# A fused attention and gated feed-forward kernel: a buffer of its own, three early sums, another order and engine table

## The chip, the cores and the metric

The kernel runs on one core of a Trainium2 chip. The metric is the device time of one launch in microseconds (us). The median of three runs of the kernel before is 399.03 us (398.22, 399.34 and 399.03).

The core's engines each work through their own queue in order: TensorE (PE in the profile; PEld are its weight loads), VectorE (DVE), ScalarE (ACT), GpSimd (POOL) and SyncE (SP). Here POOL also issues the loads, and SP most of the stores.

## The reference

Attention with a squared relu in place of the softmax, then a gated feed-forward block. Eight batches, twelve heads, 448 tokens, head size 64; model width 768, inner width 1536.

```
scores = q @ k.T / sqrt(64)
attn   = relu(scores)**2 / 448
x      = attn @ v                      # heads side by side: 3584 tokens x 768
g, val = x @ w_gate, x @ w_val
out    = (gelu(g) * val) @ w_out
```

Inputs and output are float32; the kernel computes in bfloat16 and sums in float32.

## The kernel before

**Matmuls.** All the kernel's matmuls but transposes, warm-up and fillers work on a 64 x 64 quarter of the array (`mm`, L408). A step (`Op`) is two matmuls beside each other in columns; the steps for the upper rows of the array form one lane (PE0), those for the lower rows another (PE1). When both lanes have work, four quarter matmuls run at once.

**Attention of a batch.** The heads of a batch come in six pairs, and two pairs make a third: third (b, m) is heads 4m to 4m+3 of batch b. For the first two batches PE turns q and k by transposes (`add_first_transposes` L632, `add_transposes` L658), DVE or ACT copies them out of PSUM (L647, L680). A batch has 21 scores steps u (`add_scores`, L706): PE multiplies into one of two PSUM buffers, a relu reads it (L743, ScalarE), a square follows on VectorE (L752). `add_values` (L782) multiplies by v and writes the scaled result to xT (L814 VectorE, L825 ScalarE).

**Feed-forward.** `add_gate_value` (L1040) makes one sum for 128 inner columns fc and for the gate (g = 0) or the value (g = 1): six steps in each lane over the six 128-row pieces of x, then a Gelu (L1061) or a product (L1066). The weights come in six chunks of 256 inner columns (w0 to w5), a gate and a value half each. For some columns (those of chunk 2 in batches 0 and 1) two batches are worked together by seven products in place of eight (`add_pair`, L926, with weight sums made on VectorE, L890). The output product (`add_product`, L1193) does the same for tiles of tokens. In the last two batches the products at L990 may run on GpSimd.

**Order.** The program is planned at build time. Batch 0 has a fixed order: a list of (time, step) entries, where score u stands at `lo + u * step`, so that places can be told in scores. All later work is a list of units in the order of `LINE` (L12); `run_plan` (L107) goes through time, takes the first unit that can begin, and gives each operation of ACT, DVE and GpSimd to its engine, or, where it has an alternative (`other`), to the engine that can begin first. Where the plan leaves PE idle before 30 us, `fill` (L583) puts in matmuls whose result nobody reads (L597), but only into banks that have been used before.

**Start.** A zeroed tile (L395) feeds eight pairs of warm-up matmuls (L1465). GpSimd issues the first loads and makes the identity matrix for the transposes (a memset and a mask) behind the first two.

**Loads.** All run through GpSimd's queue, in order. `LOADS` (L31) is the order after batch 0: w a weight chunk, o a quarter of the output weights, q a third of q and k, v a third of v. q and k land in a ring of two buffers (`hpool`, RING_H), v in one of three: a load waits until the transposes, or the values, of the third that used its buffer are done (L1469).

**The first batch's sums.** The gate and the value sum of fc = 0 are in batch 0's fixed list (L1045, L1371): three upper-row steps each before the last values, three behind; their lower-row steps follow later.

## Time and profile before

| | |
|---|---|
| runs of the kernel before | 398.22, 399.34, 399.03 us; median 399.03 |
| profiled execution, first to last instruction (span) | 396.5 us, mean granted TensorE clock 0.998 |
| batch 0's attention | from 5.6 to about 27.2 us of the span |
| last matmul's end, end of the span | 391.3, 396.5 us |

The profiled execution's own total isn't listed with the three runs; its span of 396.5 us leaves out what lies before the first and behind the last instruction. In the views, a line has the engine, the line of the kernel (a helper's line, where one helper issues all: L409 is every quarter matmul), the operation, what it writes and reads, its form and count, then busy us and mean ns, then idle time of the engine before it and what ended that. In rows of stages each engine has its busy us and, in brackets, its count; the last three columns are the granted clock, the DMA engines' share and GB/s. In a timeline the columns are start, length, and what ran. The chain of work that ended last is followed back from the last instruction.

### The profile page before, as it was taken

What the parts mean: (1) busy time and instruction counts of PE and PEld (TensorE: products, weight loads), DVE (VectorE), ACT (ScalarE), POOL (GpSimd) and SP (SyncE); (2) the same over time, 40 slices, a digit from 0 to 9 for tenths busy, and PEclk for the clock granted to TensorE, in tenths of its full rate; (3) what the DMA queues carried; (4) which work ended last, traced back from release to release, by engine and by line L of the source; (5) the groups of instructions that cost most, each with busy time, mean ns of one, the idle gap of its engine ahead of it and who ended that gap; (6) DMA issues with size and microseconds to landing.
All of it is one profiled execution on the core that took longest, in us unless ns stands there. A gap on an engine that the chain in (4) does not pass through costs nothing.

```text
span 396.5 us, 18486 instructions
## 1 busy us (share of the span) xinstructions
PE 388.8 (98%) x8414; PEld 329.9 (83%) x8414; DVE 313.0 (79%) x540; ACT 256.2 (65%) x388; POOL 96.5 (24%) x142
## 2 busy tenths in 40 slices
PE   8999999999999999999999999999999999999994
PEld 3555868888989997888999979999999977779993
DVE  2885897698977778889887879898988897688642
ACT  4957873787777656785776658778877465554220
POOL 8548423061230130120300402210110034341100
PEclk9999999999999999999999999999999999999999
DMA  7999999799796694573879997657523320000136
GB/s 99 180 192 175 197 195 143 96 148 155 103 233 108 113 192 71 87 95 51 110 140 150 141 196 122 89 86 120 75 30 83 94 70 4 3 2 3 41 104 180
DMA packets 75054, 44.38 MB, mean 112 GB/s; under 512 B 34400, under 2 KB 71520, under 8 KB 74976
## 3 DMA queue, kind: packets, MB, share of 16 engines
q0 software_dynamic: 38784, 24.39, 45.3%
q1 hardware_dynamic: 35792, 18.03, 22.9%
q8 instruction: 66, 1.08, 1.1%
q10 hardware_dynamic: 400, 0.79, 0.6%
q14 instruction: 12, 0.10, 0.1%
HBM read 48.76 MB, written 11.01 MB: 151 GB/s over the span
## 4 chain that ended last, share of the span: by engine, by line
PE 97%; ACT 1%; issue 0%; DVE 0%
PE ff L409 85%; PE sp L409 9%; PE ff L597 1%; PE sp L676 1%; PE ff L1465 1%; PE ff L676 1%; ACT attnT L743 1%; PE ff L639 0%; ACT qkT L647 0%; ACT osb L1267 0%; ACT xT L825 0%; DVE held L395 0%; DVE table L398 0%
## 5 line engine op out<-in xcount | busy, mean ns | idle before, releaser
L743 ACT ACTIVATE attnT<-sp 128x896 bf16<-128x896 f32 x168 | 151.3, 921 | 46.6 <-PE sp L409 44.0
L409 PE MATMUL ff<-xT,wg 64*64 64x448 bf16 x1680 | 174.5, 349 | 0.0
L409 PE MATMUL ff<-xT,wv 64*64 64x448 bf16 x1056 | 112.5, 349 | 0.0
L409 PEld LDWEIGHTS <-wv 64*64 64x64 bf16 x1680 | 93.5, 107 | 13.4 <-issue 0.6
L409 PEld LDWEIGHTS <-wg 64*64 64x64 bf16 x1680 | 93.6, 107 | 10.9
L752 DVE TENSOR_TENSOR attnT<-attnT 128x1792 bf16<-128x1792 bf16 (+1 forms) x98 | 92.2, 953 | 10.5 <-ACT attnT L743 10.0
L409 PE MATMUL ff<-attnT,v 64*64 64x448 bf16 (+1 forms) x768 | 81.5, 326 | 0.1
L409 PE MATMUL sp<-qkT 64*64 64x448 bf16 (+1 forms) x768 | 74.3, 328 | 0.9 <-ACT qkT L647 0.6
L409 PE MATMUL ff<-ts,wv 64*64 64x448 bf16 x624 | 69.3, 349 | 0.0
L409 PEld LDWEIGHTS <-s 64*64 64x64 bf16 x1200 | 66.8, 107 | 2.6 <-issue 0.2
L486 POOL DMA_DIRECT2D v<-in_v_dram x48 | 30.4, 648 | 104.2 <-ACT attnT L743 51.2
L981 DVE TENSOR_TENSOR part<-ff,part 128x448 f32<-128x448 f32 x78 | 47.0, 621 | 9.1 <-PE ff L409 6.3
L409 PE MATMUL ff<-ts,ws 64*64 64x448 bf16 x480 | 54.0, 349 | 0.0
L409 PE MATMUL ff<-wt,s 64*64 64x384 bf16 x624 | 52.1, 323 | 0.0
L409 PEld LDWEIGHTS <-uT 64*64 64x64 bf16 x912 | 50.6, 107 | 1.1
L409 PE MATMUL ff<-wo,s 64*64 64x384 bf16 x576 | 50.9, 323 | 0.0
L409 PE MATMUL ff<-wo,uT 64*64 64x384 bf16 x576 | 49.8, 323 | 0.0
L409 PEld LDWEIGHTS <-v 64*64 64x64 bf16 x768 | 44.0, 107 | 5.0 <-issue 0.9
L409 PEld LDWEIGHTS <-ws 64*64 64x64 bf16 x720 | 41.3, 106 | 5.7 <-issue 0.3
L409 PEld LDWEIGHTS <-qkT 64*64 64x64 bf16 x768 | 35.2, 106 | 9.3 <-issue 4.4
L977 ACT COPY part<-ff 128x448 f32<-128x448 f32 x54 | 28.8, 533 | 20.6 <-PE ff L409 19.4
L471 POOL DMA_DIRECT2D qk<-in_q_dram x26 | 16.5, 633 | 101.2 <-DVE attnT L752 37.7
(76 smaller groups left out, 499.7 us busy)
## 6 DMA issues: line engine op xcount, KB each, us to landing
out_dram<-osb SPq DMA_DIRECT2D x51, 192.0 KB, 3.2
v<-in_v_dram POOLq DMA_DIRECT2D x48, 128.0 KB, 4.9
qk<-in_q_dram POOLq DMA_DIRECT2D x22, 224.0 KB, 5.5
qk<-in_k_dram POOLq DMA_DIRECT2D x22, 224.0 KB, 5.8
wg<-in_moe_w_gate_dram POOLq DMA_DIRECT2D x6, 384.0 KB, 9.6
wv<-in_moe_w_val_dram POOLq DMA_DIRECT2D x6, 384.0 KB, 10.7
wo<-in_moe_w_out_dram POOLq DMA_DIRECT2D x8, 288.0 KB, 7.7
out_dram<-osb ACTq DMA_DIRECT2D x3, 192.0 KB, 3.4
```

The costliest lines, as they stand in the source:

```text
L409: return nc.tensor.matmul(o, lhsT, rhs, start=start, stop=stop, skip_group_check=onto, tile_position=(P * row, P * col))
L471: op = load(4 * (h1 - h0) * S * D, lambda: nc.gpsimd.dma_start(tile_of(), src[b, h0:h1].rearrange("h (p c) d -> p h (c d)", c=SC)), deps, ...
L486: return nc.gpsimd.dma_start(v16[b, m][HALF[i], :, :, :], v[b, h0:h1].rearrange("h (p c) d -> p h c d", c=SC)[:, :, c0:c0 + VC, :])
L597: nc.tensor.matmul(t[:, :], warm[:, 0:128], warm[:, :], start=True, stop=True)
L676: nc.tensor.transpose(t[HALF[j], c, :], src[:, 2 * r + j, c, :], ident[:, :], tile_position=(0, P * j))
L743: relu.ins = nc.scalar.activation(duo["a"][:, u % 2, :, :], box[0][:, :, 0:S], AF.Relu).ins
L752: nc.vector.tensor_tensor(a[:, part], a[:, part], a[:, part], op=ALU.mult)
L977: rd.ins = copy(st["t", name][:, :], box[0][:, 0:S]).ins
L981: rd.ins = nc.vector.tensor_tensor(t[:, :], box[0][:, 0:S], t[:, :], op=ALU.add).ins
L1465: nc.tensor.matmul(t[HALF[j], :], warm[:, HALF[j]], warm[:, :], start=True, stop=True, tile_position=(0, P * j))
```

## The change

It has these parts.

- **Start.** The warm-up reads the constant 1.0 instead of the zeroed tile and has ten pairs instead of eight. `fill` may also use a bank that nothing has used yet, and counts on half the pace before 7.2 us; it thus adds a matmul ahead of the first scores. The identity's memset goes to VectorE, its mask behind the second pair of loads.
- **Own buffer.** q and k of third (0, 2) land in a tile of another pool (`lpool`) and take no turn in the ring of two; the turns of all later thirds move up by one.
- **Loads.** `LOADS` now names each load; the order is another one.
- **Three early sums.** Gate of fc 0, gate of fc 1 and value of fc 0 stand in batch 0's list, with a place for each step (`SUMS_AT`: fc, g, lane that goes first, six places in scores). The sum of fc 1 does its lower rows first.
- **Order.** Batch 0's transposes and values have places of their own (`TURN_AT`, `VALUE_AT`), and `LINE` is another order of the same units.
- **Engines.** More operations have an alternative: relus of the first two batches (VectorE), squares (ScalarE, in batch 0 GpSimd for every third u), copies of batch 0's transposes and xT (ScalarE), the copies that regroup q and k (ScalarE). A table, `CHOICE`, says for each of 373 operations whether it stays (0), goes to the other engine (1), or is left to the plan (a dot). In order of the operations the table begins with batch 0's 21 relus, `1010.00.001.01...000.`; for batch 0 it fixes the squares of u = 8, 9 and 14 on ScalarE and that of u = 13 on GpSimd and leaves eight open; for batches 1 to 7 it fixes 14 squares on ScalarE.
- **The plan's figures.** Durations, load times and start times in the plan are other ones, and it keeps VectorE and GpSimd apart for some operations. These act through the order alone. (`NP4`, `SPANS`, `BY_DVE`, `ALONE_FROM` and `SOON_V` have values that change nothing.)

A copy of both transposes of a third in batch 1 and later also waits for both, not for its own alone.

The diff, cut to its core:

```diff
-w q q w q v q w v w w v w q v q o v q o q v o o q v v q v v v q q v q v q v q q q v v q q v v q q v
-v v
+w0 q10 q11 w1 w5 q12 v10 v12 v11 w3 w4 q20 q21 v20 w2 v21 q22 o3 q30 o2 q31 o1 v22 o0 v31 q32 v30
+q40 v32 v40 q41 q42 q51 q50 v41 v50 v42 v51 q52 v52 q60 v60 q61 q62 q70 v62 v61 q71 q72 v70 v72 v71
...
+TURN_AT = (-1.3, 2.0, 4.2, 6.5, 11.2, 13.5)
+VALUE_AT = (7.2, 9.2, 13.2, 16.2, 19.2)
+TURN1_AT = 23.61
+SUMS_AT = ((0, 0, 0, 18.4, 20.7, 21.0, 22.8, 23.0, 25.5), (1, 0, 1, 21.0, 21.2, 22.0, 22.0, 23.3, 27.8), (0, 1, 0, 21.0, 21.1, 21.8, 21.9, 24.8, 25.75))
...
+    nc.vector.memset(ident[:, :], 0.0)
...
+    def qk_tile(b, m):
+        if (b, m) not in qk16:
+            home, name = (lpool, "qkr") if (b, m) == (0, 2) else (hpool, "qk16")
+            qk16[b, m] = home.tile([128, 4, SC * D], bf16, name=name, tag=name)
+        return qk16[b, m]
...
-        if t1 > FILL:
+        if t1 > FILL or not held:
             return
-        at_rest = {k: -1.0 if r is None else r.end for k, r in held.items() if r is None or r.end is not None}
+        at_rest = {k: -1.0 if held.get(k) is None else held[k].end for k in range(FB)
+                   if held.get(k) is None or held[k].end is not None}
...
-        n = int((t1 - t0 - 0.15) / 0.22)
+        n = int((t1 - t0 - 0.15) / (0.22 if t1 > COLD else 0.43))
...
-        relu = Op("ACT", 0.845, emit_relu, [ops[0][-1], ops[1][-1]], lag=0.18, prio=2)
+        relu = Op("ACT", 0.845, emit_relu, [ops[0][-1], ops[1][-1]], lag=0.18, prio=2,
+                  other=("DVE", 1.0, emit_relu) if b < EARLY else None)
...
+            sq = Op("DVE", 0.575 if alone else 1.05, emit_sq, [relu] if alone else duo["relu"], lag=0.2, prio=2,
+                    other=("GPS", 1.75, lambda: emit_sq(nc.gpsimd)) if aside
+                    else ("ACT", 0.85 if alone else 1.5, lambda: emit_sq(nc.scalar)))
...
-        if h0 == 0:
-            POOL.append(Op("POOL", 0.6, lambda: make_identity(nc, ident)))
+        if h0 == 2:
+            POOL.append(Op("POOL", 0.3, lambda: make_identity(nc, ident, nomemset=True)))
...
-    work += [(0.0, 5, add_gate_value, (0, 0, g)) for g in range(2)]
+    soon = {(0, fc, g): (fore, *(lo + x * step for x in at)) for fc, g, fore, *at in SUMS_AT}
+    for key, at in soon.items():
+        work.append((at[1], 5, lambda t, key, end: kept.__setitem__(key, take_bank(t, end - t + 12.0)), (key, at[-1])))
+        work.append((0.0, 5, lambda _, key, at: add_gate_value(at, *key), (key, at)))
...
     def emit_warm_up():
+        ones = nc.const_aps.tensor(1.0, (128, 512), bf16)
         t = new_bank(0, None)
-        for _ in range(8):
+        for _ in range(10):
             for j in range(2):
-                nc.tensor.matmul(t[HALF[j], :], warm[:, HALF[j]], warm[:, :],
+                nc.tensor.matmul(t[HALF[j], :], ones[:, HALF[j]], ones,
...
-        for new, old in zip(thirds[ring:], thirds):
+        turns = [x for x in thirds if made is not qk_loads or x != (0, 2)]
+        for new, old in zip(turns[ring:], turns):
...
+    either = [op for op in [*ACT, *DVE, *SP] if op.other is not None]
+    free_to = {"ACT": [*ACT], "DVE": [*DVE], "GPS": [*GPS], "SP": [*SP]}
+    picks = "".join(CHOICE.split()) or [op.choice for op in either]
+    for op, pick in zip(either, picks):
+        op.choice = pick
+        if pick == "1":
+            free_to[op.engine].remove(op)
+            op.engine, op.cost, op.emit = op.other
+        if pick != "0":
+            free_to[op.other[0]].append(op)
```

More of the change, by code (lines that the diff above doesn't have):

```diff
@@ L52, in __init__ @@
         self.open = False
+        self.choice = "."
+        self.port = self.full = False
+        self.first = engine, cost
 class Ring:
@@ L104 @@
 ALONE = True
+BEGIN = {"PE0": 1.2, "PE1": 1.2, "POOL": 1.25, "GPS": 1.25, "ACT": 2.3, "DVE": 1.4, "SP": 0.75}
+MOVED = 0.0
 def run_plan(queues, pools, units, banks, arrivals, together, fill):
-    free = {e: 0.0 for e in (*queues, *pools)}
+    free = {e: BEGIN.get(e, 0.0) for e in (*queues, *pools)}
     at = {e: 0 for e in queues}
-    dma = last = floor = busy = alone = 0.0
+    dma = MOVED
+    last = floor = busy = alone = 0.0
+    port = {"DVE": 0.0, "GPS": 0.0}
     fixed = len(queues["PE0"])
@@ L282, in run_plan @@
         free[e] = op.end
+        if op.full:
+            free["PE1"] = op.end
+        if op.port and e in port:
+            port[e] = op.end
+        if e in ("POOL", "GPS"):
+            free["POOL"] = free["GPS"] = op.end
         if e in together:
@@ L1082, in add_gate_value @@
         bank_read(box["k"], done)
-        then(at, GS, *ops, box, lambda: done, ("g", b, fc, g))
+        if fore:
+            for i, hi in enumerate(ops[1]):
+                if i:
+                    hi.after = ops[1][i - 1]
+                pairs.append(("at", at[i], hi))
+            ops[0][0].deps.append(ops[1][-1])
+            later.append(Unit(("g", b, fc, g), ops[0], []))
+        else:
+            then(at, GS, *ops, box, lambda: done, ("g", b, fc, g))
         if later and later[-1].name == ("g", b, fc, g):
@@ L1440 @@
     for kind, lo, hi in pairs:
-        if kind == "with":
+        if kind == "at":
+            upper.append((tau[sum(t <= lo for t, _ in lower)], hi))
+        elif kind == "with":
             upper.append((tau[place[lo]], hi))
```

215 lines of the change are left out of this document (131 added, 84 removed).

## The prediction

> **What bounds the kernel now.** First the page: the busy shares, and the chain of work that ended last, by line.
>
> ```profile
> span 396.5 us, 18486 instructions
> ...
> PE 388.8 (98%) x8414; PEld 329.9 (83%) x8414; DVE 313.0 (79%) x540; ACT 256.2 (65%) x388; POOL 96.5 (24%) x142
> ...
> PE ff L409 85%; PE sp L409 9%; PE ff L597 1%; PE sp L676 1%; PE ff L1465 1%; PE ff L676 1%; ACT attnT L743 1%; PE ff L639 0%; ACT qkT L647 0%; ACT osb L1267 0%; ACT xT L825 0%; DVE held L395 0%; DVE table L398 0%
> ```
>
> TensorE (PE) is the bound: 98% busy, and the chain is matmuls. But busy time also counts fillers (L597) and stretches in which only one of two lanes runs. So the second view is the busy time by stage, and the third gives, from the chain in order of time, how dense matmuls run.
>
> ```profile
> 5.60:27.20 21.60, 20.91 (x305) 10.92 (x305) 17.66 (x32) 17.89 (x22) 11.85 (x18) 1.00 1.28 179
> 27.20:60.00 32.80, 32.42 (x662) 23.26 (x664) 26.03 (x39) 22.66 (x32) 16.70 (x25) 1.00 1.35 187
> 60.00:380.00 320.00, 320.00 (x7188) 284.06 (x7184) 263.65 (x457) 211.26 (x327) 63.45 (x88) 1.00 0.61 99
> ```
> ```profile
> 11.18 0.51 PE ff L676 x14
> ...
> 69.97 1.70 PE ff L409 x36
> ...
> 309.69 81.58 PE ff L409 x1805
> ```
>
> The dense pace is 36 matmuls of 448 columns in 1.70 us, 0.0472 each (four run side by side); 14 transposes take 0.51. I take half, 0.024, for 224 columns. Now the matmuls by form in stage A, batch 0's attention (5.6 to 27.2):
>
> ```profile
> L597 PE MATMUL ff<-held 128*128 128x512 bf16 x17 | 5.2, 384 | 0.0
> L409 PE MATMUL ff<-attnT,v 64*64 64x224 bf16 x24 | 3.2, 260 | 0.1
> L676 PE MATMUL ff<-ident,qk 128*64 128x128 bf16 x70 | 2.9, 222 | 0.0
> L409 PE MATMUL sp<-qkT 64*64 64x224 bf16 x24 | 1.2, 265 | 0.0
> ```
>
> Of 305 matmuls, 17 are fillers, 48 half ones and 84 transposes (70 here, and the 14 that PE's timeline has at 5.61, below); 156 full ones are left. 156 x 0.0472 + 48 x 0.024 + 6 x 0.51 = 7.4 + 1.1 + 3.1 = 11.6 us of useful work in 21.6: **10.0 us are lost**. Stage B (27.2 to 60) has 112 transposes (L676) and again 48 half matmuls:
>
> ```profile
> L676 PE MATMUL sp<-ident,qk 128*64 128x128 bf16 x112 | 4.5, 222 | 0.0
> L409 PE MATMUL ff<-attnT,v 64*64 64x224 bf16 x24 | 3.0, 256 | 0.0
> L409 PE MATMUL sp<-qkT 64*64 64x224 bf16 x24 | 1.3, 257 | 0.0
> ```
>
> 502 x 0.0472 + 1.1 + 8 x 0.51 = 28.9 of 32.8: **3.9 us are lost**. From 60 to 380 PE is busy without a gap, and the chain's last long piece is 81.58 us in one go. So the time is a fixed amount of matmul work, the start, these 14 us, and the tail. The change can win from the first three alone.
>
> Stage A is held not by PE but by ScalarE's relus (groups in that window, then ScalarE's timeline):
>
> ```profile
> L743 ACT ACTIVATE attnT<-sp 128x896 bf16<-128x896 f32 x21 | 17.4, 933 | 1.2 <-PE sp L409 1.2
> ```
> ```profile
> 30.52 0.92 ACT L743 ACTIVATE attnT<-sp 128x896 bf16<-128x896 f32 x1 [5.15 <-PE sp L409]
> ```
>
> 21 relus, 17.4/21 = 0.83 apart, with 1.2 idle, end at 30.52 - 5.15 = 25.4; then ScalarE waits 5.15 us for batch 1's first scores. Stage B is held by what has been loaded. The DMA view from 5 to 60 us, two rows of GpSimd's (POOL's) timeline, and the time to landing of these issues:
>
> ```profile
> DMA packets 17254, 10.08 MB, mean 183 GB/s; under 512 B 697, under 2 KB 17244, under 8 KB 17244
> ```
> ```profile
> 42.76 0.62 POOL L486 DMA_DIRECT2D v<-in_v_dram  x1 [1.43 <-DMA wv<-in_moe_w_val_dram]
> ...
> 45.00 0.83 POOL L449 DMA_DIRECT2D wv<-in_moe_w_val_dram  x1 [0.80 <-issue]
> ```
> ```profile
> v<-in_v_dram POOLq DMA_DIRECT2D x2, 128.0 KB, 11.4
> ```
> ```profile
> wv<-in_moe_w_val_dram POOLq DMA_DIRECT2D x1, 384.0 KB, 13.0
> ```
>
> The last value-weight chunk lands at 45.0 + 13.0 = 58.0, the last third of batch 1's v about 42.8 + 11 = 54. Until then batch 1's attention isn't complete.
>
> **The change part by part.** *Start.* PE's and POOL's timelines:
>
> ```profile
> 1.19 3.62 PE L1465 MATMUL ff<-held 128*64 128x512 bf16 x16 [1.19 <-DVE table L398]
> 4.88 0.58 PE L597 MATMUL ff<-held 128*128 128x512 bf16 x1
> 5.61 0.67 PE L639 MATMUL ff<-ident,qk 128*64 128x128 bf16 x14
> 6.84 0.57 PE L409 MATMUL sp<-qkT 64*64 64x448 bf16 x8 [0.57 <-ACT qkT L647]
> ```
> ```profile
> 0.31 0.10 POOL L1542 MEMSET const-bfloat16-1.0<- 128x1 bf16 x1
> ```
> ```profile
> 2.60 0.23 POOL masks.py:197 MEMSET ident<- 128x128 bf16 x1
> 2.91 0.29 POOL masks.py:199 TENSOR_SCALAR_AFFINE_SELECT ident<-ident 128x128 bf16<-128x128 bf16 x1
> ```
>
> The warm-up no longer waits for VectorE's (DVE's) memsets but for a constant that is there at 0.41; it starts between 0.4 and 1.19. Ten pairs at 3.62/8 = 0.45 end between 4.9 and 5.7, and the filler of 4.88 has no room. The first transposes begin between 5.1 (the filler out of their way) and 5.8, against 5.61. Between them and the first scores, in the gap from 6.28 to 6.84, the new filler fits or costs 0.1. More unbroken work may bring full pace sooner: the first 14 transposes took 0.67 for a later 0.51, the eight first scores 0.57 for 8 x 0.0472: 0 to 0.3. Bounds -0.3 and +0.8; I take **0.2 gained**, near no change. The identity's memset of 0.23 moves to DVE, idle then, and its mask of 0.29 behind two loads: loads three and four go out 0.52 sooner, later ones 0.23. The mask is still done by 4. As the transfers are back to back, this is inside those bounds.
>
> *Own buffer and load order.* POOL issues in order, so a load that waits for a buffer holds all behind it:
>
> ```profile
> 20.29 0.61 POOL L471 DMA_DIRECT2D qk<-in_q_dram  x1 [3.88 <-PE ff L676]
> ```
>
> This is batch 1's second q/k third, behind 3.88 us for transposes of (0,2). Now thirds (0,2) and (1,0) find free buffers, and (1,1) waits for transposes of (0,1), some eight scores earlier. But transfers run throughout, so issuing sooner is worth nothing by itself; the order is. A weight chunk is 768 KB, a q/k third 448, a v third 256; 183 GB/s are 179 KB per us. Before, 7168 KB end with chunk 5 at 58.0, so they began at 18.0. In the new order w0 q10 q11 w1 w5 come first (3200 KB: 35.9), then q12 v10 v12 v11 (4416: 42.7, not 54), w3 w4 (5952: 51.3), and behind three more thirds w2 (7872: 62.0), which only the paired sums need. All chunks of batch 0's plain sums are there at 51, not 58, and batch 1's values can end some 8 us sooner, if its relus follow. Of stage B's 3.9 I take **1.8 gained**, between bounds of 0 and 3.5. Late next are w2 and the output weights, behind batch 1's plain sums: 5 chunks x 4 sums x 24 matmuls x 0.0472 = 23 us.
>
> *Three early sums.* A sum is 12 steps of two matmuls. Before, two sums began inside stage A (six steps each); now three, one of them in the other lane, from score 18 on, beside fillers and single-lane matmuls. Six more steps are 12 x 0.0472 = 0.57, and steps beside a lane that ran alone may save as much again. Bounds 0 (PE would only wait longer for w1) and 1.1: **0.6 gained**. No other engine gets work from it.
>
> *Engines by table (CHOICE).* It isn't in the short description: some of batch 0's relus go to DVE, some squares to ScalarE and GpSimd, transposes' and xT's copies either way. No such relu or square is in this trace; the nearest rows:
>
> ```profile
> L752 DVE TENSOR_TENSOR attnT<-attnT 128x1792 bf16<-128x1792 bf16 x70 | 75.8, 1087 | 9.2 <-ACT attnT L743 8.9
> L981 DVE TENSOR_TENSOR part<-ff,part 128x448 f32<-128x448 f32 x78 | 47.0, 621 | 9.1 <-PE ff L409 6.3 <-ACT part L977 2.2
> ```
> ```profile
> L990 POOL TENSOR_TENSOR uT<-gel,part 128x448 bf16<-128x448 bf16 x16 | 17.6, 1107 | 65.0 <-ACT gel L985 55.9 <-DVE part L981 9.1
> ```
>
> A relu on DVE is between 0.62 and 1.24; I take 1.1. A ScalarE square of 896 elements I put beside its relu, 0.9; a GpSimd one between 1.1 and 2.2. Batch 0 has two score buffers, so two relus side by side don't double the pace: a buffer's turn is a relu of 0.9 to 1.1 plus waits and matmuls of about 0.7 (6.28 to 6.84 shows 0.56 of waits for a copy), every two relus: 0.8 to 0.9 apart, against 0.83. The pace stays; of the 1.2 idle and the copies behind the last relu I take **0.6 gained**, bounds -0.8 and 1.5.
>
> A rule of the Trainium skill speaks against this: page "SBUF — State Buffer", section "Who interferes with whom", says that a two-input VectorE instruction and a GpSimd instruction reading SBUF lock each other out. By it one to four squares hold DVE up to 2.2 each, and the 0.6 would be -0.5. No row here shows who waited beside the 16 GpSimd products.
>
> *Later stages.* The same matmuls, where PE has no gap to lose; new order and choices can only open some: 0 to 1, I take 0.2 lost. **Sum:** 0.2 + 1.8 + 0.6 + 0.6 - 0.2 = 3.0; the span becomes 393.5. Around the span lie 2.5 (the runs' median of 399.03 less 396.5; the profiled execution's own total isn't listed), kept: **396.0**.
>
> **Rivals.** *Moved, not saved:* early sums empty the stock that PE lives on until w1, which comes at 18.0 + 2432/179 = 31.6 before and after, and batch 1 stays paced by its relus. For it speaks ScalarE's idle 5.15; against, w5 and v sooner. The start's 0.2 and half of stage A's 1.2 remain: 398.2. Chance 0.16.
>
> *Slower, ScalarE late with evictions:* the table fixes 14 squares of batches 1 to 7 on ScalarE, 1.1 (DVE's row) to 1.9 (two relus) each, ahead of reads that free PSUM banks. Were half of them 1 us late for PE, 7 us are lost: 403.0. It decides where ScalarE is over 95% busy for more than 5 us; from 60 to 380 it is at 211/320 = 66%, which speaks against. Chance 0.08.
>
> *Table reloads:* the trace has one table load for Relu, Copy and Gelu together.
>
> ```profile
> L399 ACT ACT_TABLE_LOAD x1 | 1.3, 1283 | 0.7 <-PEq L1542 0.7
> ```
>
> Were squares to need another table, 17 among Gelus would cost 34 x 1.283 = 44 us of ScalarE; half of that on the path gives 418. The Trainium skill, page "ScalarE: Activation LUTs", section "Table sets: the hidden batching unit", names relu, copy, identity and abs as in every set, and not square; no row here shows one. Chance 0.03.
>
> **How the numbers follow.** The forecast's case has 0.73. Its better bounds together would give over 6 us; 5.6 of them are the range's low end, 393.4. Upward it takes in the moved case with half a us of new gaps, 398.7. Left out are the slower cases (0.11) and some 0.08 beyond the ends. A measurement of this kernel tells 0.3%, 1.2 us, from no change. The forecast's case is faster by more, the moved case within, the last two slower: 0.73, 0.16, 0.11.
>
> **What would show it.** Right: first relu before 7.2; batch 0's relus over 17 to 18 us; fewer than 14 fillers after the warm-up; under 2.5 us lost from 27 to 60; chunk 5 landed near 36, batch 1's v near 43, w2 near 62; one table load. Wrong: gaps on PE after 60, a loss still near 4 in stage B, or ScalarE full for long stretches.

## The result, and the profile after

The changed kernel took 402.33 us (median of 6 runs, 401.14 to 402.80) where the kernel before took 398.57 beside it (6 runs): a ratio of **1.0090, 95% interval 1.0073 to 1.0107**, slower by 0.9%. The forecast was 396.0, faster. (A ratio leaves out the few executions that took over 1.5% longer than the fastest of their kernel; a median has all.) The profiled execution of the changed kernel took 402.8 us, the longest of the six; its page begins so, and its chain of work that ended last has a new member:

```profile
span 400.9 us, 18481 instructions
...
PE 93%; DMA 3%; ACT 1%; DVE 1%; issue 0%; POOL 0%; ACTq 0%; POOLq 0%
PE ff L448 82%; PE sp L448 8%; DMA v<-in_v_dram 2%; PE ff L646 1%; DMA qk<-in_k_dram 1%; PE sp L726 1%; ACT attnT L803 1%; PE ff L726 1%; POOL qk L517 0%; DVE osb L1352 0%; DVE s L1263 0%; DVE osb L1354 0%; ACT osb L1354 0%; ACTq L1373 0%; ACT xT L893 0%
```

Before, PE was 97% of this chain and no DMA stood in it; now the load of v is 2%, 7.45 us in the list of the chain. (L448 is every quarter matmul, L646 the fillers.) By stage, with the same accounting as in the prediction:

```profile
5.20:27.20 22.00, 20.71 (x311) 11.02 (x314) 18.77 (x28) 18.82 (x24) 17.33 (x23) 1.00 1.30 183
27.20:60.00 32.80, 32.60 (x685) 25.19 (x686) 26.34 (x37) 24.12 (x30) 14.82 (x22) 1.00 1.36 189
60.00:380.00 320.00, 315.99 (x7060) 286.27 (x7055) 258.90 (x460) 231.00 (x320) 63.67 (x89) 0.99 0.61 96
```

Stage A's matmuls by form, those that don't count as full ones:

```profile
L646 PE MATMUL ff<-held 128*128 128x512 bf16 x16 | 5.0, 385 | 0.0
...
L448 PE MATMUL ff<-attnT,v 64*64 64x224 bf16 x24 | 3.2, 262 | 0.1
L726 PE MATMUL ff<-ident,qk 128*64 128x128 bf16 x42 | 1.7, 222 | 0.3 <-DMA qk<-in_k_dram 0.3
L448 PE MATMUL sp<-qkT 64*64 64x224 bf16 x24 | 1.5, 260 | 0.0
L726 PE MATMUL ff<-ident,qkr 128*64 128x128 bf16 x28 | 1.2, 222 | 0.0
...
L688 PE MATMUL ff<-ident,qk 128*64 128x128 bf16 x14 | 0.6, 220 | 0.2 <-PE ff L1561 0.2
```

And stage B's:

```profile
L448 PE MATMUL ff<-attnT,v 64*64 64x224 bf16 x22 | 3.4, 257 | 0.1
L726 PE MATMUL sp<-ident,qk 128*64 128x128 bf16 x84 | 3.1, 221 | 0.0
L448 PE MATMUL sp<-qkT 64*64 64x224 bf16 x24 | 1.7, 256 | 0.0
```

Stage A has 311 - 16 - 48 - 84 = 163 full matmuls: 7.7 + 1.1 + 3.1 = 11.9 us of useful work in 22.0, **10.1 lost** (before 10.0). Stage B has 685 - 46 - 84 = 555: 26.2 + 1.1 + 3.1 = 30.4 of 32.8, **2.4 lost** (before 3.9). The start ends at 5.2, not 5.6. So up to 60 us, by these two profiles, the change gained 0.4 - 0.1 + 1.5 = 1.8 us, of 3.2 forecast. The span grew by 4.4 all the same: 6.2 us were lost after 60, where PE had lost nothing. Of these, 3.6 are one wait, here in the view of waits from 60 on:

```profile
PE ff L448 <- DMA v<-in_v_dram: 3.6, 1, 3.6
```

Some 1.7 more lie right behind it, in the granted clock (third figure from the end of a row):

```profile
120.30:122.00 1.70, 1.70 (x27) 1.33 (x31) 0.69 (x2) 1.27 (x2) 0.00 (x0) 0.66 1.17 261
122.00:124.00 2.00, 2.00 (x29) 1.64 (x24) 1.63 (x2) 0.55 (x2) 0.00 (x0) 0.50 1.20 211
124.00:126.00 2.00, 2.00 (x48) 1.44 (x44) 0.47 (x1) 1.45 (x3) 0.00 (x0) 0.93 0.18 24
```

0.34 x 1.70 + 0.50 x 2.00 + 0.07 x 2.00 = 1.7. "Busy" is 100% in these rows; only the clock and the count of matmuls (27 in 1.70 us, where 36 were dense) show the loss. The wait and its echo are 5.3 of the 6.2; another 0.4 stands behind the last matmul, which ends 5.6 us before the span does (at 395.3), against 5.2 before.

What was late is v of third (3,0), read from 116.7 on. GpSimd's timeline, after and then before (L532 and L486 issue v, L517 and L471 q and k):

```profile
110.36 1.26 POOL L532 DMA_DIRECT2D v<-in_v_dram  x2 [19.13 <-ACT attnT L803]
111.60 0.63 POOL L517 DMA_DIRECT2D qk<-in_q_dram  x1
112.20 0.64 POOL L517 DMA_DIRECT2D qk<-in_k_dram  x1
112.81 1.36 POOL L532 DMA_DIRECT2D v<-in_v_dram  x2
```
```profile
106.49 0.66 POOL L471 DMA_DIRECT2D qk<-in_q_dram  x1 [16.07 <-DVE attnT L752]
107.14 0.62 POOL L471 DMA_DIRECT2D qk<-in_k_dram  x1
107.75 2.47 POOL L486 DMA_DIRECT2D v<-in_v_dram  x4
```

`LOADS` had `q32 v30 v31` and now has `v31 q32 v30`: two loads are issued ahead that PE needs later. Moreover the whole burst starts 3.9 us later. Before, v of (3,0) had landed by 113.1 and was read at 115.75; after, it was issued at 112.81 and landed at 120.3 and 121.2. PE's first read of it before:

```profile
115.75 0.35 PE L409 MATMUL ff<-attnT,v 64*64 64x448 bf16 x2
```

Of the 3.9 us, 1.2 stood when the DMA transposes ahead of the burst began (98.63 before, 99.84 after). The other 2.7 arose in these transposes, which took 10.0 us to their last landing (109.80), where they had taken 7.3 (105.93). Why they took longer is not shown.

### The profile page after: what moved, and what is told of

Its sections match the earlier page's. It is cut to its first block, busy times and chain, and to the rows that moved or that the text cites. A ratio compares the mean times of both kernels' runs of the same rounds, so it can differ in the third digit from the quotient of the medians.

```text
span 400.9 us, 18481 instructions
## 1 busy us (share of the span) xinstructions
PE 388.9 (97%) x8416; PEld 337.6 (84%) x8416; DVE 312.6 (78%) x544; ACT 278.3 (69%) x382; POOL 99.9 (25%) x144
## 3 DMA queue, kind: packets, MB, share of 16 engines
q8 instruction: 66, 1.08, 1.1%
## 4 chain that ended last, share of the span: by engine, by line
PE 93%; DMA 3%; ACT 1%; DVE 1%; issue 0%; POOL 0%; ACTq 0%; POOLq 0%
PE ff L448 82%; PE sp L448 8%; DMA v<-in_v_dram 2%; PE ff L646 1%; DMA qk<-in_k_dram 1%; PE sp L726 1%; ACT attnT L803 1%; PE ff L726 1%; POOL qk L517 0%; DVE osb L1352 0%; DVE s L1263 0%; DVE osb L1354 0%; ACT osb L1354 0%; ACTq L1373 0%; ACT xT L893 0%
## 5 line engine op out<-in xcount | busy, mean ns | idle before, releaser
L448 PE MATMUL ff<-xT,wg 64*64 64x448 bf16 x1680 | 177.3, 350 | 0.3 <-ACT xT L893 0.2
L803 ACT ACTIVATE attnT<-sp 128x896 bf16<-128x896 f32 x155 | 140.8, 916 | 41.3 <-PE sp L448 38.8
L448 PE MATMUL ff<-xT,wv 64*64 64x448 bf16 x1056 | 115.6, 349 | 0.0
L448 PEld LDWEIGHTS <-wg 64*64 64x64 bf16 x1680 | 96.8, 107 | 11.2 <-issue 1.1
L448 PEld LDWEIGHTS <-wv 64*64 64x64 bf16 x1680 | 97.2, 106 | 9.6 <-issue 0.8
L448 PE MATMUL ff<-attnT,v 64*64 64x448 bf16 (+1 forms) x768 | 85.8, 329 | 3.7 <-DMA v<-in_v_dram 3.6
L448 PE MATMUL sp<-qkT 64*64 64x448 bf16 (+1 forms) x768 | 73.0, 329 | 0.7 <-DVE attnT L801 0.4
L448 PE MATMUL ff<-ts,wv 64*64 64x448 bf16 x624 | 71.3, 349 | 0.0
L448 PEld LDWEIGHTS <-s 64*64 64x64 bf16 x1200 | 67.8, 108 | 3.1 <-issue 0.2
L814 DVE TENSOR_TENSOR attnT<-attnT 128x1792 bf16<-128x1792 bf16 (+1 forms) x66 | 62.7, 959 | 6.6 <-ACT attnT L803 6.2
L532 POOL DMA_DIRECT2D v<-in_v_dram x48 | 30.2, 642 | 114.0 <-ACT attnT L803 46.9
L448 PE MATMUL ff<-ts,ws 64*64 64x448 bf16 x480 | 54.8, 349 | 0.0
L448 PEld LDWEIGHTS <-uT 64*64 64x64 bf16 x912 | 52.1, 107 | 2.9 <-issue 0.7
L448 PE MATMUL ff<-wt,s 64*64 64x384 bf16 x624 | 54.3, 326 | 0.0
L448 PEld LDWEIGHTS <-v 64*64 64x64 bf16 x768 | 46.4, 107 | 8.8 <-DMA v<-in_v_dram 4.0
L448 PE MATMUL ff<-wo,uT 64*64 64x384 bf16 x576 | 52.7, 323 | 0.0
L448 PE MATMUL ff<-wo,s 64*64 64x384 bf16 x576 | 52.7, 324 | 0.0
L812 ACT ACTIVATE attnT<-attnT 128x1792 bf16<-128x1792 bf16 (+1 forms) x30 | 44.9, 1500 | 1.3 <-DVE attnT L801 0.7
L448 PEld LDWEIGHTS <-ws 64*64 64x64 bf16 x720 | 42.7, 106 | 3.5
L448 PEld LDWEIGHTS <-qkT 64*64 64x64 bf16 x768 | 35.9, 106 | 7.8 <-issue 3.7
L517 POOL DMA_DIRECT2D qk<-in_q_dram x25 | 16.1, 646 | 82.6 <-ACT attnT L803 32.9
```

The costliest lines, as they stand in the source:

```text
L448: return nc.tensor.matmul(o, lhsT, rhs, start=start, stop=stop, skip_group_check=onto, tile_position=(P * row, P * col))
L517: op = load(4 * (h1 - h0) * S * D, lambda: nc.gpsimd.dma_start(qk_tile(b, m)[HALF[i], r0:r0 + h1 - h0, :], src[b, h0:h1].rearrange("h (p c ...
L532: return nc.gpsimd.dma_start(v16[b, m][HALF[i], :, :, :], v[b, h0:h1].rearrange("h (p c) d -> p h c d", c=SC)[:, :, c0:c0 + VC, :])
L803: relu.ins = nc.scalar.activation(at, sp, AF.Relu).ins
L812: engine.activation(a[:, part], a[:, part], AF.Square)
L814: engine.tensor_tensor(a[:, part], a[:, part], a[:, part], op=ALU.mult)
```

## The experiments

Each run was timed beside the kernel before. "Sooner" or "later" at a place compares the same instruction of ScalarE in two profiles; the order of work is the same in all versions of the changed kernel.

**1. v of (3,0) first.** The planned order stays; only the two loads change places where they are issued:

```diff
+    early_v, late_v = ([op for op in POOL if getattr(op, "token", None) == ("v", x)] for x in ((3, 0), (3, 1)))
+    for a, c in zip(early_v, late_v):
+        a.emit, c.emit = c.emit, a.emit
```

> The changed kernel with one thing different: the loads of the first and second third of batch 3's v change places in GpSimd's queue, so that v of (3,0) is issued at about 110.4 instead of 112.8 us and lands near 114, ahead of the values that read it at about 116.5. Theory (the loss is one late load): TensorE's 3.6 us of idle time before those values goes, and with it the 2 us that a granted clock of 0.50 to 0.66 costs behind it; 5.6 us less, about 396.7 us, a ratio to the kernel before near 0.995, and the clock column stays at 1.00 from 110 to 130. Rival (the order of the work, or the engine table, costs the time and the wait only shows where): another wait takes its place, the time stays within 1 us of 402.3.

399.52 us, ratio 1.0026 (1.0005 to 1.0048): 2.8 us better, where 5.6 were expected. The stretch itself did what the theory says: PE full from 116 to 120.3, clock 1.00, and ScalarE's instructions at 127 were 5.5 us sooner against those of the changed kernel than at 115.8. But 1.3 us were lost again by 137, and 0.9 more had been lost at 88, where the profile names no cause. First the window of the old wait, then the wait that stood behind it:

```profile
116.00:120.30 4.30, 4.30 (x107) 4.25 (x101) 3.80 (x7) 3.55 (x6) 0.62 (x1) 1.00 1.29 221
```
```profile
PE sp L448 <- DMA qkT<-qkr: 0.9, 1, 0.9
```

Scores of (3,2) wait for DMA transposes which may begin only when the burst of loads ahead of them has landed. In the changed kernel the longer wait had hidden this one.

**2. A busy wait.** Seventeen matmuls whose result nobody reads go ahead of the late values:

```diff
+                if (b, pr) == (3, 0):
+                    ones = nc.const_aps.tensor(1.0, (128, 512), bf16)
+                    for _ in range(17):
+                        nc.tensor.matmul(box[0][:, :], ones[:, 0:128], ones, start=True, stop=True)
```

> The changed kernel with 17 matmuls of 128x512 more, whose result nobody reads, ahead of the late values of (3,0): the wait for the load stays, but TensorE is busy in it. Theory (the price of the wait is the wait and then a lowered clock that follows from the idle time): the granted clock stays at 1.00 from 120 to 126, the 448-column matmuls behind the wait stay at about 0.35 us and not 0.58, and 2 us are won: about 400.3 us, ratio to the kernel before near 1.004. Rival A (the low clock has nothing to do with the idle time): the clock falls as before and the time stays at 402.3. Rival B (the added matmuls themselves hold the work up): slower than 402.3.

The clock did as the theory says; in the same windows as above:

```profile
120.30:122.00 1.70, 1.70 (x46) 1.47 (x42) 0.79 (x3) 1.30 (x2) 0.00 (x0) 1.00 1.22 293
122.00:124.00 2.00, 2.00 (x54) 1.46 (x50) 1.84 (x3) 1.83 (x3) 0.00 (x0) 1.00 0.83 133
```

Work behind the wait came 1.5 us sooner. The time did not follow: 404.04 us (ratio 1.0144, 1.0117 to 1.0171), 1.7 more than the changed kernel. Two further v loads were late for the earlier PE, at 264 and 288 (2.7 us in the view of waits), and ScalarE's instructions there fell 3.3 us back. So the rows show the echo's price, and in this run winning it back won nothing. That the loads, being behind, took the gain away is argued from the two late loads; why the loss was larger than the gain is open.

**3. v of (3,0) second** (v of (3,1), v of (3,0), then q and k of (3,2)).

```diff
+    tokens = ("v", (3, 1)), ("q", (3, 2)), ("v", (3, 0))
+    turn = [op for x in tokens for op in POOL if getattr(op, "token", None) == x]
+    emits = [op.emit for op in turn]
+    for op, n in zip(turn, (0, 1, 4, 5, 2, 3)):
+        op.emit = emits[n]
```

> The changed kernel with the order v of (3,1), v of (3,0), then q and k of (3,2): v of (3,0) is issued 1.2 us sooner than in the changed kernel and 1.2 later than with v of (3,0) first, and should land between 115.5 and 119. A dose between the two. Theory (the time follows the landing of this one load): idle time before the values between 0 and 2.5 us, a lowered clock only if some of it is left, 397 to 400 us, between the run with v of (3,0) first and the changed kernel. Rival (it isn't the landing but what else shares the stretch, four stores and q and k of (3,2)): no ordering by the landing; with q and k last another wait, for the regrouped q and k, appears and the time is as long as the changed kernel's.

399.64 us, ratio 1.0035 (1.0013 to 1.0058): as good as first place. The profile has no wait for v and no lowered clock; instead 1.1 us for DMA transposes near 134, 0.9 for output weights near 101 and 0.9 near 126, where no cause is named. But it shows one of the slower executions, 402.43 us, in which batch 0 ended late (see 9) and PE came to v of (3,0) 3.2 us later than in the changed kernel, at 119.58. The loads landed at 119.14 and 120.56; a PE that was not late might have waited for them. So the median, inside the forecast's range, fits the theory, but that the load was in time in the usual execution is not shown. The rival's new wait came as well; the median did not go back to 402.

**4. The kernel before with v of (3,0) late** (behind v of (3,1) and q and k of (4,0)), a control.

```diff
+    tokens = ("v", (3, 0)), ("v", (3, 1)), ("q", (4, 0))
...
+    for op, n in zip(turn, (2, 3, 4, 5, 0, 1)):
+        op.emit = emits[n]
```

> The kernel before, with one thing different: v of (3,0) goes behind v of (3,1) and the q and k of (4,0) in its burst, as it stands behind two others in the changed kernel. In the kernel before it landed at 112.43 and 113.11, and is read at about 115.8; in its new place the loads landed at 115.60 and 117.37. Theory (a late v of (3,0) alone makes the loss): TensorE waits 1 to 2 us for it near 116, less than the 3.6 of the changed kernel, and the time grows by 1 to 2 us: 399.5 to 400.5, a ratio of 1.002 to 1.005; the granted clock falls little or not at all. Rival (the wait shows only in the changed order of work): within 0.5 us of the kernel before.

403.31 us, ratio **1.0102** (1.0066 to 1.0137): this order alone, in the kernel before, costs as much as the whole change, and more than expected, since the loads landed at 120.5 and 121.6 in place of 117.4.

```profile
PE ff L409 <- DMA v<-in_v_dram: 3.1, 1, 3.1
```

**5. Fewer loads ahead of the transposes** (v of (3,0) first, and q and k of (4,0) and v of (3,2) issued behind the transposes of (3,2)).

```diff
         def paced():
+            if getattr(op, "token", None) in (("q", (4, 0)), ("v", (3, 2))) and "turned" not in held_back:
+                held_back.setdefault("loads", []).append(paced)
+                return
...
             turned.append(ins)
+            if (b, m, c1) == (3, 2, SC):
+                held_back["turned"] = True
+                for late_load in held_back.get("loads", ()):
+                    late_load()
```

> The run with v of (3,0) first still had a wait at 130 us that the changed kernel had hidden behind its longer one: scores of (3,2) waited 0.9 us for DMA transposes that landed at 130.90, which began at 125.65, when the last load of the burst ahead of them (q and k of (4,0), v of (3,2)) had landed at 125.52. Here these four loads are issued behind the transposes of (3,2) in place of ahead of them, besides v of (3,0) first. Theory (the new load order leaves the alternation of loads and transposes short of time): the transposes begin near 120 and land near 125, the wait at 130 goes, about 1.1 us less than with v of (3,0) first, 398.4 us, a ratio near 1.000. Rival A (margins are thin everywhere): v of (3,2) or the transposes of (4,0) are late instead, between 135 and 145, and the time stays at 399.5 or grows. Rival B (the gaps after 60 are chance, another place each time): the time stays within 0.5 of 399.5.

405.43 us, ratio 1.0168 (1.0144 to 1.0191): worse. The transposes landed at 125.6 and the wait at 130 was gone, but VectorE's copy that regroups q and k of (4,0) now waited for its load, and the squares behind it in VectorE's queue waited too. VectorE's timeline and PE's wait:

```profile
131.60 0.63 DVE L564 COPY qkr<-qk 128x1792 bf16<-128x1792 bf16 x1 [7.19 <-DMA qk<-in_k_dram]
132.14 0.55 DVE L1363 COPY osb<-ff 128x384 f32<-128x384 f32 x1
132.61 1.08 DVE L823 TENSOR_TENSOR attnT<-attnT 128x1792 bf16<-128x1792 bf16 x1
```
```profile
PE ff L448 <- DVE attnT L823: 5.8, 1, 5.8
```

Rival A, at another place than it named: what waits is an engine's queue, not the load's reader alone.

**6. o3 ahead of v of (2,1),** 50 us ahead of the stall. The profiles' DMA share from 60 to 64 us, before and after (share of 16 engines and GB/s are the last two columns), and GpSimd's timeline after:

```profile
60.00:62.00 2.00, 2.00 (x48) 1.51 (x43) 1.59 (x4) 0.74 (x2) 2.00 (x4) 1.00 1.15 163
62.00:64.00 2.00, 2.00 (x49) 1.74 (x44) 2.00 (x3) 0.55 (x1) 0.58 (x1) 1.00 1.02 144
```
```profile
60.00:62.00 2.00, 2.00 (x57) 1.48 (x52) 1.17 (x3) 0.80 (x2) 0.32 (x1) 1.00 0.68 71
62.00:64.00 2.00, 2.00 (x50) 1.47 (x46) 1.75 (x5) 1.20 (x2) 2.00 (x4) 1.00 0.51 52
```
```profile
56.69 0.63 POOL L532 DMA_DIRECT2D v<-in_v_dram  x1 [2.66 <-ACT attnT L803]
59.12 0.61 POOL L532 DMA_DIRECT2D v<-in_v_dram  x1 [1.80 <-DVE attnT L801]
61.68 0.61 POOL L517 DMA_DIRECT2D qk<-in_q_dram  x1 [1.94 <-PE sp L726]
62.28 0.97 POOL L517 DMA_DIRECT2D qk<-in_k_dram  x1
63.24 1.50 POOL L503 DMA_DIRECT2D wo<-in_moe_w_out_dram  x2
```

The new order puts v of (2,1) ahead of the output weights (wo), which wait for nothing. Its two loads wait, as the rows say, for relus (ACT L803, DVE L801): beside the ring of buffers the kernel, before and after, has a rule of its own by which a load of v also waits for relus of the third two places earlier (L1577). So it is this pacing that holds the queue, not a busy buffer, which the expectation below takes it for. The q and k of (2,2) wait for themselves as well, for PE's transposes (1.94 at 61.68); only the output weights are held needlessly. The queue stands, the transfers run dry, and from there the kernel's own rule (a transpose waits for the last load issued ahead of it, a load for the last transpose) makes one chain of loads and transposes without a pause. The first transposes begin at 69.64 before and 71.36 after. The edit:

```diff
+    tokens = ("v", (2, 1)), ("q", (2, 2)), ("o", 3)
...
+    for op, n in zip(turn, (4, 5, 0, 1, 2, 3)):
+        op.emit = emits[n]
```

> The changed kernel with one thing different, far ahead of the wait: the last quarter of the output weights (o3) is issued ahead of v of (2,1), not behind it and q and k of (2,2). In the changed kernel GpSimd's queue waits at 56.7 and 59.1 us for a free v buffer, o3 stands behind that until 63.2, and the transfers fall to 71 and 52 GB/s between 60 and 64; the first DMA transposes then begin at 71.36, against 69.64 in the kernel before, and from there loads and transposes follow each other without a pause up to 125. Theory (the loads fell behind in that hole, and the late v of (3,0) is its end): o3 fills the hole, the first transposes begin 3 to 5 us sooner, the burst that holds v of (3,0) sooner too, so that its loads land near 116 to 118 and the 3.6 us of idle time shrink to less than 1.5, with no lowered clock: 397.5 to 399.5 us. Rival (only the place of v of (3,0) in its own burst counts; later bursts are released by relus, not by the chain of transfers): the burst is issued at 110 as before and the time stays at 402.3.

398.89 us, ratio 1.0013 (0.9985 to 1.0041): **3.4 us better with v of (3,0) still last of the three.** The time is the theory's. In its profile (402.87 us, the longest of its executions, see 9) the transfers carry 184 and 210 GB/s there, and there is no wait for v near 116, but 1.1 us of waits for v near 288 and 290. In this execution PE was 2.75 us late from batch 0 on and read v of (3,0) at 120.04; but the loads had landed at 116.73 and 117.39, so that a PE in time, at 117.3, would hardly have waited either. How much sooner the chain of transfers runs shows better in run 7, which has the same edit and no late batch 0.

**7. Both load changes** (the edits of 1 and 6).

> Both: o3 ahead of v of (2,1), and v of (3,0) ahead of v of (3,1). Theory (loads behind by two to four us from 71 on are the common cause of the waits at 116 and at 130): with the chain of transfers sooner the wait at 130 for DMA transposes (0.9 us with v of (3,0) first alone) goes too, and what is left of the gain up to 60 us shows: 396.5 to 398.5 us, ratio to the kernel before between 0.995 and 1.000. Rival (other gaps take their place, as in every version up to now): 399 to 400 us, as with v of (3,0) first alone (399.5).

398.30 us, ratio **0.9977** (0.9950 to 1.0003). The first transposes begin at 66.84 (71.36 in the changed kernel), the burst with v of (3,0) at 104.65 (110.36), and the view of waits from 60 to 390 has nothing but

```profile
PE ff L448 <- issue: 0.2, 1, 0.2
```

Loads are no longer waited for in this execution (396.84 us, 1.5 below the median; span 395.1). This version beats the changed kernel by 1.0%; from the kernel before it is not told apart.

**8. The engine table in batch 0,** and **9. GpSimd's squares,** each beside v of (3,0) first:

```diff
-            if relu.engine == "DVE":
+            if relu.engine == "DVE" and b:
...
+            engine = engine if b else nc.vector
```
```diff
+            engine = nc.vector if engine is nc.gpsimd else engine
```

> As the run with v of (3,0) first, and besides batch 0's relus all run on ScalarE and its squares all on VectorE, in the order and at the places of the changed kernel. The prediction counted 0.6 us gained from the engine table in batch 0 (between -0.8 and 1.5): by it this run is 0.6 us slower than the run with v of (3,0) first. What the trace of the changed kernel suggests instead is that the table lengthens batch 0's chain (first relu 6.82 to last relu's end at about 26.0, 19.2 us, against 18.1 in the kernel before): by that the last relu ends about 1 us sooner here, and the total is the same to 1 us shorter. A third reading, that the chain's length doesn't matter because stage B takes it up: the relus end sooner and the total stays within 0.3 us.

> As the run with v of (3,0) first (399.5), and besides batch 0's two GpSimd squares run on VectorE. In one profile (v of (3,0) second) a VectorE square took 2.87 us beside a GpSimd square of 1.73, and batch 0 ended 2.5 us later than in the changed kernel; in the other profiles they missed each other. Theory (the two engines hold each other up when a two-input product meets a GpSimd one, and that happens in some executions): the runs scatter less and their median is 0.3 to 1 us lower, 398.5 to 399.2. Rival (GpSimd's squares unload VectorE, which has eleven squares, six relus and copies in batch 0): the chain of batch 0 gets longer by up to 1 us and the time is 399.5 to 400.5.

In run 8 batch 0's relus and squares are back on their old engines; the copies stay where the table puts them. 400.21 us, ratio 1.0049 (1.0027 to 1.0071), 0.7 above run 1 with intervals that overlap. Batch 0's relus go from 6.78 to 26.79 (20.0 us) without the table; with it, in run 1, from 7.32 to 26.38 (19.1). The last relus of each, ScalarE's timeline without the table and with it:

```profile
20.80 5.99 ACT L803 ACTIVATE attnT<-sp 128x896 bf16<-128x896 f32 x7
```
```profile
23.01 3.37 ACT L803 ACTIVATE attnT<-sp 128x896 bf16<-128x896 f32 x4 [0.39 <-PE sp L448]
```

In these two profiles the table shortens the chain by 0.9 us. It does not in every execution: of the eight profiles that have the table, GpSimd's squares and ten pairs, six have a chain of 19.1 to 19.7 us and two one of 21.5 and 22.9 (see 9); their mean is 20.0, as without the table. So neither a gain nor a loss by the table is shown. Without GpSimd's squares alone: 399.24 us, ratio 1.0017 (0.9999 to 1.0035), not told apart from run 1. What made it worth trying is in the profile of run 3, VectorE's row and GpSimd's:

```profile
19.99 2.87 DVE L814 TENSOR_TENSOR attnT<-attnT 128x896 bf16<-128x896 bf16 x1
```
```profile
20.64 1.73 POOL L814 TENSOR_TENSOR attnT<-attnT 128x896 bf16<-128x896 bf16 x1
```

The same square takes 0.61 elsewhere. It happened in 2 of 9 profiles with these squares (runs 3 and 6), where batch 0 ended 2.5 to 3.6 us later. The prediction cited a rule for this from the Trainium skill, page "SBUF — State Buffer", section "Who interferes with whom": a VectorE instruction with two inputs in SBUF and a GpSimd one that reads SBUF lock each other out. The traces agree in part. In the four profiles without GpSimd's squares no VectorE square of this form took over 0.63, and relus on VectorE (one input) beside a GpSimd square stayed at 1.08 to 1.09. But in all nine profiles a VectorE square also runs into GpSimd's first square and is not held up; in the changed kernel's two such squares take 1.15 together, and the second ends 0.36 us inside GpSimd's:

```profile
13.00 1.15 DVE L814 TENSOR_TENSOR attnT<-attnT 128x896 bf16<-128x896 bf16 x2
```
```profile
13.79 1.91 POOL L814 TENSOR_TENSOR attnT<-attnT 128x896 bf16<-128x896 bf16 x1
```

And in run 3 the square that is held up begins 0.65 us ahead of GpSimd's, more than its usual 0.61. So two engines that meet don't always hold each other up, and what sets the two long squares apart is not shown.

Both load changes without GpSimd's squares (the edits of 1, 6 and 9):

> As the run with both load changes, and batch 0's two GpSimd squares on VectorE, as the run that did this (399.24 against 399.52, not told apart). Theory (the two engines held each other up in some executions): 0.2 to 0.4 us below the run with both, and a narrower spread. Rival (no difference but the longer chain on VectorE): equal or up to 0.6 longer.

398.87 us, ratio 0.9999 (0.9973 to 1.0024): no gain over run 7 that can be told.

**10. The start.** The warm-up on the zeroed tile again, beside v of (3,0) first (the edit below turned round); the kernel before with the constant, with eight pairs and with ten:

```diff
+        ones = nc.const_aps.tensor(1.0, (128, 512), bf16)
...
-                nc.tensor.matmul(t[HALF[j], :], warm[:, HALF[j]], warm[:, :],
+                nc.tensor.matmul(t[HALF[j], :], ones[:, HALF[j]], ones,
```

> As the run with v of (3,0) first (399.5), but the warm-up reads the zeroed tile, as in the kernel before, still ten pairs. The prediction took 0.2 us for the start, between -0.3 and 0.8. Theory (the start's gain comes from the warm-up that doesn't wait): it begins at about 1.2 and not 0.78, the first relu comes 0.4 us later than in the run with v of (3,0) first and so does the end of batch 0, and the time is 0.2 to 0.5 us longer. Rival (the filler, or the load of q and k of the first third, sets the first scores): first relu within 0.1 us, the time within 0.2.

> The kernel before with the constant read by the warm-up (eight pairs as before), nothing else. The prediction took 0.2 us for the start, between -0.3 and 0.8; in the changed kernel the warm-up that reads the tile again put the first relu 0.46 us later in the profile. Theory (the start is worth that by itself): the first relu comes before 7.0 instead of at 7.27, the time is 0.2 to 0.5 us below the kernel before. Rival (the mask of the identity or the first load holds the first transposes): first relu within 0.1 us of 7.27, the time within 0.2.

> The kernel before with the constant read by the warm-up, and ten pairs in place of eight, as in the changed kernel. Theory (the two added pairs hold the first transposes): against the run with the constant and eight pairs (first relu 6.54, 397.8 us) the first relu comes 0.3 to 0.6 us later, near 7.0, and the time is 0.2 to 0.5 longer, 398.0 to 398.3. Rival (they keep the array at full pace): the first relu within 0.1 of 6.54 and the time equal.

The old warm-up: first relu 0.46 later (7.78), 399.82 us, ratio 1.0021 (1.0001 to 1.0041), not told from run 1. The constant in the kernel before: 397.80 us, ratio 0.9982 (0.9959 to 1.0005), the first relu at 6.54, not 7.27. With ten pairs: 398.11 us, ratio 0.9986 (0.9974 to 0.9997, just below 1), first relu at 7.36. One profile's first relu is a weak measure, though: the ten profiles of the changed kernel and its variants with constant and ten pairs have it anywhere from 6.53 to 7.37. With the tile it came at 7.27, 7.56 (run 4) and 7.78, with the constant and eight pairs at 6.54 to 6.56 in three profiles. So the constant tends to bring it forward and eight pairs leave it early, as the theories said; by how much is not shown, and a difference in time between eight and ten pairs can't be told. PE's timeline with eight:

```profile
4.30 0.38 PE L597 MATMUL ff<-held 128*128 128x512 bf16 x1
4.96 0.58 PE L639 MATMUL ff<-ident,qk 128*64 128x128 bf16 x14 [0.28 <-DMA qk<-in_k_dram]
```

The load of k is late next. Both load changes with eight pairs (`range(10)` becomes `range(8)`), and that without GpSimd's squares:

> As the run with both load changes (398.3 us, ratio to the kernel before 0.9977), with eight pairs of warm-up matmuls in place of ten. In the kernel before with the constant alone the first transposes began at 4.96, held by the load of k, and the first relu at 6.54; in the changed kernel ten pairs end at 5.09 to 5.26 and the transposes begin at 5.24 to 5.41. Theory (the two added pairs hold the first transposes and give back part of what the constant brings): transposes near 5.0, first relu 0.3 to 0.4 us sooner, 0.3 us less in all: about 398.0. Rival (without them the array is colder and the first transposes and scores run slower): the first relu isn't sooner, the time 398.3 or more.

> As the run with both load changes and eight pairs, and batch 0's two GpSimd squares on VectorE. In two of nine profiles a VectorE square took 2.87 us, not 0.61, beside GpSimd's second square, and batch 0 ended 2.5 to 3.5 us later. Theory (that happens in some executions and costs them 2 us or more): no VectorE square of 896 elements takes over 1 us, and of twelve runs fewer lie over 400 us than without this edit; median 0.2 to 0.5 us lower, 397.5 to 397.8. Rival (the spread has another cause; the squares unload VectorE): the same spread, the median equal or up to 0.5 higher.

398.36 us, ratio 0.9998 (0.9968 to 1.0028), and 398.06, 0.9996 (0.9977 to 1.0014): nothing won. The first relu came 0.5 sooner than in run 7's profile, and by 10 us the work was 1.5 to 1.6 later: PE waited 0.96 (0.75 in the other) for the next load of k, and in both the granted clock fell. Windows of the first of the two:

```profile
7.00:8.00 1.00, 0.36 (x9) 0.39 (x11) 0.97 (x2) 0.64 (x1) 1.00 (x3) 0.87 1.14 165
8.00:9.00 1.00, 1.00 (x12) 0.40 (x7) 0.28 (x1) 0.42 (x1) 1.00 (x3) 0.50 1.03 136
9.00:10.00 1.00, 1.00 (x7) 0.27 (x6) 0.35 (x1) 0.48 (x1) 1.00 (x2) 0.50 1.17 144
```

Of twelve executions, three were over 400 us with GpSimd's squares and none without; with ten pairs (run 7 and run 9's second version) it was one with them and two without. That the squares make the spread is not shown.

## Why the prediction was wrong, step by step

- **Later stages** is the step that failed: "The same matmuls, where PE has no gap to lose; new order and choices can only open some: 0 to 1, I take 0.2 lost". It was 6.2, of which the wait for v of (3,0) and the lowered clock behind it are 5.3. The step looked at PE, which was full, and not at how closely its loads arrived: 115.75 - 113.1 = 2.7 us of margin for v of (3,0). The order of loads was followed up to w2 and no further; `v31 q32 v30` stood in the diff, and what a waiting load holds behind it on GpSimd's queue was named for batch 1 only. Run 1 in the changed kernel and run 4 in the kernel before show that the place of this load makes the loss; run 6, with the load's place unchanged, that it was late also because the loads had fallen behind at 60 already.
- **Stage B** (1.8): right, 1.5 measured. Chunk 5 landed at 35.6, batch 1's v by 41.9, w2 at 60.3, near the 36, 43 and 62 of the prediction. But the same order is what ran the transfers dry at 60: the gain in B and the loss at 116 are parts of one edit, which run 7 takes apart.
- **Start** (0.2): not measurable. The first relu came at 6.82 for 7.27, but equal starts differ by up to 0.8 from profile to profile. In time the constant alone gave 0.9982 (0.9959 to 1.0005), an interval that holds the 0.2 as well as nothing at all.
- **Engines by table** (0.6): not shown. The prices were near: 1.09 for a relu on VectorE (1.1 taken), 0.95 for a ScalarE square (0.9), 1.71 to 1.91 for a GpSimd one (1.1 to 2.2). Batch 0's chain is 0.9 us shorter with the table in one pair of profiles and equal in the mean of eight; the medians' 0.7 is not told apart. A long VectorE square beside GpSimd's exists (2 of 9 profiles); the prediction's row-based value left it out.
- **Three early sums** (0.6): stage A as a whole gained nothing (-0.1). "The pace stays" was wrong: batch 0's relus take 20.0 us in the new order on the old engines (run 8) and took 18.1 in all four profiles with the old order. The sum has no term for the new places of batch 0's transposes and values. Which part of the order lengthens the chain (these, or the third sum) was not tried apart.
- **Around the span** (2.5): mis-sized by some 0.7. In every execution on record 1.7 to 1.9 us lie between span and time; the profiled one thus took some 398.3, less than the median of 399.03 that it was set against.
- **Rivals.** "Moved, not saved" is out in the profile: 1.8 us were there at 60. "ScalarE late with evictions" had the right direction, slower by something late after 60, and the wrong cause: the wait was for a load. No table reload: one load of 1.3 us as before. The sign that would refute, "gaps on PE after 60", is the one that came; "fewer than 14 fillers" (16) and "relus over 17 to 18 us" (from 6.82 to 26.07, 19.2) failed as well.

With both load changes (run 7) the profiled span is 1.4 below the kernel before, against 3.0 forecast; but that execution was 1.5 faster than its median, and the medians differ by 0.3 us, the ratio 0.9977 not told from 1. What is left of the 1.8 us in a usual execution is not shown, nor were the new `LINE` and the table of the later batches tried apart.

## What to carry to other kernels

A queue with loads in order has one more bound than its engines: for every load after the edited stage, compare its landing with its first reader, and for every load that waits, for a buffer or by a rule of the kernel's own, ask what is queued behind it. An engine that is full tells nothing of that margin. And a wait that is removed shows the next one, so a repair is priced by what stands behind it.

## What the runs showed of the hardware

- **The clock after an idle wait.** PE idle for 3.62 us (changed kernel): granted clock 0.50 for some 3.4 us from just behind it (0.66, 0.50 and 0.93 in the rows above). Idle for 5.79 us (run 5): 0.50 for some 6.8 us, which began inside the wait. Idle for 3.12 us (run 4): 1.00 throughout. The Trainium skill, page "TensorE: Matmul & The Clock Gate", section "Part 1: The HAM clock gate (the "warmup" mystery)", has the array fall to half its clock after an idle window of about 3.4 us; these three agree. But in the run with eight pairs waits of 0.55, 0.24 and 0.96 between 4.4 and 7.6 us came before 0.50 from 8 to 11, and 0.60, 0.24 and 0.75 did in that without GpSimd's squares: near the start, broken work preceded it too. Waits of 0.28 and 0.57 (eight pairs in the kernel before) did not.
- **Matmuls in a wait keep the clock** (run 2): 1.00 behind it, where it had fallen to 0.50.
- **A load issued behind others in a burst takes longer to land:** in the changed kernel's burst the first load of v took 3.5 us from issue to landing (110.36 to 113.86), that of v of (3,0), with four loads ahead, 7.4 (112.81 to 120.25), the last 9.8. Before, with two loads ahead, v of (3,0) took 4.7. What the stores beside them cost is not shown.
